# The sixteen matmuls of the masked products with r, alternating between the two column halves of TensorE's array

## The chip, the cores and the metric

The kernel runs on one core of one Trainium2 chip. Five engines work side by side: TensorE (PE in the profile, with its weight loads listed as PEld), VectorE (DVE), ScalarE (ACT), GpSimd (POOL) and SyncE (SP), which here issues all the DMAs. The metric is the device time of one execution in microseconds; less is better.

## The reference

The input passes through a recurrence, and then through two feed-forward blocks. The recurrence is, for 4 batches x 8 heads and for each of 768 steps (head size 40):

```
y[:, :, t] = einsum('bhd,bhde->bhe', rt, state)
Sa = einsum('bhde,bhe->bhd', state, at)
state = state * wt[:, :, None, :] - einsum('bhd,bhe->bhde', Sa, bt) + einsum('bhd,bhe->bhde', vt, kt)
...
x = y as [3072, 320];  h = (x @ w1) * (x @ w2) @ w3;  x = h @ w_out
h = maximum(x @ w_in, 0);  out = (h * h) @ w_out2
```

Inputs are float32 (the weights of the feed-forward blocks arrive in 64 bits and are cut to float32 on the chip).

## The kernel before, in words

The recurrence runs in 24 chunks of 32 steps (`C = 32`), one after the other, all 32 pairs of batch and head at once. What a chunk needs that does not depend on the state is prepared six chunks ahead. The state is then carried from chunk to chunk by six stages of TensorE, each of which writes one PSUM tile that another engine empties before the next stage can run:

- `do_x0` (matmuls at L723): state times a; ScalarE empties it (L725).
- `do_sa` (L733): times the inverse of a triangular matrix; ScalarE empties it (L735).
- `do_sat` (L740): transposes; ScalarE empties it (L742) into the tile `vs`. For a pair of heads `vs` holds 104 rows (two heads of 40, the second from row 64 on) by 64 columns: 32 steps of v and 32 steps of Sa.
- `do_l` (L753), the stage that is changed: for each of 16 pairs of heads one float32 matmul, with 104x64 of `vs` as the weights and 104x64 of r (`RT`: 32 steps for each of the two heads) as the moving operand. The 64x64 products go through a causal mask on VectorE (L755) into rows 64 to 127 of the tile `YI`.
- `do_z` (L763): the state transposed; ScalarE empties it (L766).
- `do_ys` (L778): for each of the 32 heads the products of `YI` with `YR`, 40 columns of weights, 72 moving columns. They give the chunk's output (L790) and the next state (L786). Two heads of a pair go to two column halves of the array.

A float32 matmul appears in the trace as two records, each with its own weight load, so a block of 16 such matmuls has 32 records. A transpose appears as one.

All stages of the recurrence take their PSUM tile from one pool of two buffers, `psat()`, in turn. A stage therefore waits until the tile of the stage but one before it has been emptied. Before the change `do_l` takes two tiles, one for each 8 pairs; `do_z` comes two tiles after the first of them, and so takes that one's buffer.

Between the stages TensorE is given other work, so that it does not stand idle while another engine empties a tile: `Fill.pull(gap)` takes matmuls from a list until their estimated time has reached the gap's. In the first four chunks the list holds the product that folds two weights into one (L455); later it holds the first feed-forward block, 256 tokens for every two chunks (L366 `ab` and L424 `px`). One `ab` tile is emptied by ScalarE (`a_sb`, L397) and VectorE (`g`, L398), and there are two `ab` tiles. The preparation six chunks ahead (`prep_pq` at L578, `prep_kb` at L595, the scans `suf` L539 and `wi` L549 on VectorE) goes between the stages as well, and after every fourth preparation VectorE solves four chunks' triangular matrices in 31 pairs of instructions (`tmp` L637, `T` L640). After the recurrence comes the second feed-forward block (L366 `ph`, L971 `po`).

The order on TensorE is the program's own (`manual_schedule`). The order on the other engines and in the DMA queue is set by a scheduler that simulates a timeline and goes by priorities.

Of the kernel before, what the change touches and what calls it, by code (L numbers as in the profile page):

```python
# [7 lines left out]
F32 = mybir.dt.float32  # L8
F32R = mybir.dt.float32r
# [7 lines left out]
C = 32  # L17
# [8 lines left out]
LEAST, MOST = 0.25, 2.0  # the decays that the recurrence by chunks is meant for  # L26
# the order of the work on what the first chunks need: before the recurrence, and between its stages
# [4 lines left out]
BETWEEN = {  # by chunk and stage  # L32
# [16 lines left out]
FOLD_NS = 535  # of a product of the fold  # L49
# [4 lines left out]
# nanoseconds of other work after each stage of a chunk: x0, sa, sat, l, z, pq, kb, ys  # L54
# [13 lines left out]
FIRST, SECOND = 40000, 20000  # priorities over what comes earlier in the program  # L68
TWIN = [list(range(4 * i, 4 * i + 4)) for i in range(NCH // 4)]  # chunks solved together


class Fill:
    """Work that goes between the stages of the recurrence, in order, with about how long it holds the tensor engine."""
# [6 lines left out]
    def push(self, *items, before=None):  # L80
        """Items of (ns, function, kind); ahead of the first one of a kind, if there is one."""
        at = next((i for i, it in enumerate(self.q) if it[2] == before), len(self.q))
        for it in items:
            self.q.insert(at, it)
            at += 1
# [14 lines left out]
def general(tc, raw, w1, w2, w3t, wo, win, wo2, ident, out):  # L100
    """The same for any decays: the recurrence step by step, and the rest in float32."""
# [3 lines left out]
    with (  # L105
# [59 lines left out]
        with tc.tile_pool(name="g_w", bufs=1) as wp:  # L165
            is64 = w1.dtype != F32

            def fetch(dst, src):
                """Rows of a weight in float32."""
# [73 lines left out]
def body(tc, img, rv, rd, vn, vp, raw, w1, w2, w3t, wo, win, wo2, ident, maskt, out, dbg=None):  # L243
# [4 lines left out]
    with (  # L248
# [5 lines left out]
        X2_d = dram.tile([NCH, 128, DM], F32, name="X2_d")  # per chunk (batch, channel % 32), (channel // 32, step)  # L254
# [6 lines left out]
        with right, tc.manual_schedule(engines={mybir.EngineType.PE}):  # L261
            wp = right.enter_context(tc.tile_pool(name="wp", bufs=1, side="right"))
            wf_ = {n: wp.tile([128, 8, DM], F32R, name="wp" + n) for n in "hl"}  # the folded weight
# [6 lines left out]
            def staged(pl, tags):  # L270
                """The raw weights that come first lie where the first product will need the space."""
                slots, n = staging.setdefault(tags, (deque(), [0]))
                if not slots:
                    t = pl.tile([128, 4, 512], U32, name="early", tag=tags[n[0] % len(tags)])
                    n[0] += 1
                    slots.extend(t[:, i] for i in range(4))
                return slots.popleft()
# [12 lines left out]
            hold = []  # the end of the first window's solution: what follows on that engine waits for its turn  # L290
            count = {"fold": 0, "split": 0}  # raw weights so far
            bufs = {"raw": WB[0], "wst": WB[1], "split": WB[2]}

            def fetch(pl, K, N, parts, dst=None, tag="fold"):
                """[128, K, N] of a weight in float32; one of 64 bits is cut to it from its bits."""
# [26 lines left out]
                # as float32 the upper word has an eighth of the exponent: less 112 it is that of the float32, and  # L322
                # what is below float32's range comes close to zero by itself
# [10 lines left out]
            def split_w(pl, src, h, l, j, k):  # L334
                """Rows 128*k.. and columns 256*j.. of a [320, .] weight as a float32r sum."""
# [5 lines left out]
            def split_r(pl, two):  # L341
                """Rows 256.. of two blocks of 256 columns as float32r sums, their terms above one another: the first
                one's upper term in the lower half, the second one's in the upper half."""
# [25 lines left out]
            def a_tile(n):  # L369
                """The tokens of two chunks."""  # L370
# [68 lines left out]
            def fold(solved):  # L439
                """The weights of the first product; the steps of the fold, in pieces of 256 rows of the transposed w3."""  # L440
# [49 lines left out]
            with (  # L490
# [21 lines left out]
                def first(c, name, shape, places):  # L512
                    """A tile of a preparation; the first ones lie where later tiles will, so that they don't wait."""
# [21 lines left out]
                def prep_scan(c):  # L535
# [8 lines left out]
                    # one too small for an inverse, which `within` doesn't let pass, counts as 1  # L544
# [58 lines left out]
                TT = {}  # L603

                def solve(k, blocks):
                    """All of T by substitution, or the blocks of 16 on its diagonal alone, both at once."""
# [10 lines left out]
                    def view(x):  # L617
                        """Rows and columns of each block; the second one lies 16 rows and 16 columns on."""
# [41 lines left out]
                def corner(c, i):  # L660
                    """The block below the diagonal: - T_22 P_21 T_11, transposed, in two steps."""
# [85 lines left out]
                def do_l(c):  # L747
                    """The masked products of V_s and of SA_s with R_t."""
                    vs = vs_t.pop(c)
                    for g in range(2):  # L750
                        ps = psat()
                        for i in range(8):
                            mm(out=ps[64:128, 0, 64 * i:64 * i + 64], lhsT=vs[0:104, 8 * g + i], rhs=RT[0:104, :, 8 * g + i],  # L753
                               start=True, stop=True, tile_position=(0, 64))
                        dve.tensor_tensor(out=YI[64:128, 16 * g:16 * g + 16, 0:C],  # L755
                                          in0=ps[64:128, 0].rearrange("p (u t) -> p u t", t=C),
                                          in1=msk[64:128].unsqueeze(1).to_broadcast([64, 16, C]), op=ALU.mult)

                def do_z(c):
                    """The state, decayed over the chunk, with the rows and columns exchanged."""  # L760
# [82 lines left out]
                RT = at.tile([128, 2, 16, C], F32, name="RT", tag="rt")  # of each parity in a column of its own  # L843
# [95 lines left out]
        with (  # L939
# [39 lines left out]
            NW = 8  # pieces of the decays  # L979
# [3 lines left out]
            def look(i):  # L983
                """The least and the largest of a piece of the decays."""
# [6 lines left out]
            def within():  # L991
                """1 where all decays are such that the products of a chunk's and their inverses are far from the ends
                of the range, and 0 elsewhere."""
# [41 lines left out]
def layout(r, k, v, w, a, b, moe_w1, moe_w2, moe_w3, moe_w_out, moe2_w_in, moe2_w_out):  # L1035
    import numpy as np

    def e2(x):
        # [chunk, (parity, channel) padded to 104 rows, batch, head pair, step]
# [49 lines left out]
```

## Time and profile before

| | |
|---|---|
| three runs | 1135.08, 1135.51 and 1135.98 us, median 1135.51 |
| span of the profiled execution, first to last instruction | 1131.3 us |
| around the span (median less span) | 4.2 us |
| TensorE busy | 952.6 us (84%) |
| VectorE busy | 745.7 us (66%) |
| L753, matmuls of `do_l` | 768 records, 57.8 us busy |
| L778, matmuls of `do_ys` | 1536 records, 57.4 us busy |

Busy time is the time in which at least one instruction of the kind is under way. Matmuls overlap, so the time that a block of them holds TensorE is read from the start of its first record to the start of the next other matmul, not from the records' own durations. The granted clock (PEclk) is given as a share of 2.4 GHz; its two levels are 1.2 and 2.4 GHz.

### The profile page before, as it was taken

The page shows a single profiled execution, that of the slowest core. Times are in us where ns is not written, and L with a number is a line of the kernel's source. Part 1 is how long each engine was busy: PE and PEld are TensorE (multiplying, and loading weights), DVE is VectorE, ACT ScalarE, POOL GpSimd, SP SyncE. Part 2 cuts the span into 40 slices and gives each one's busy share as a digit, 9 for nine tenths or more (in the row PEclk, how much of TensorE's full clock was granted, in tenths as well). Part 3 has the DMA queues.
Part 4 walks back from the last instruction along what each step waited for, and adds up shares of the span by engine and source line. Part 5 has one row for each costly group of instructions (what it writes and reads, how often), then busy time and mean ns, then how long its engine had stood idle before and what let it go on. Part 6 is the DMA issues. An engine that isn't in the chain of part 4 may idle for free.

```text
span 1131.3 us, 29668 instructions
## 1 busy us (share of the span) xinstructions
PE 952.6 (84%) x12240; PEld 856.6 (76%) x12240; DVE 745.7 (66%) x1467; ACT 453.5 (40%) x1022; POOL 273.8 (24%) x310
## 2 busy tenths in 40 slices
PE   1336776688979889978899998988989999999995
PEld 1235554577879888978789898877778998889985
DVE  6795799965885796678569543789943434343332
ACT  3433655442424333333334343667433433343331
POOL 0383557622132122112210000487400000000000
PEclk9999788898999898988999998999999999999998
DMA  8878666475566655645664453449600200000000
GB/s 209 262 214 219 189 168 189 115 196 146 131 151 160 170 142 140 181 117 150 154 147 111 105 116 87 101 144 201 160 24 1 52 1 24 1 24 1 22 3 26
DMA packets 212677, 134.47 MB, mean 119 GB/s; under 512 B 142974, under 2 KB 187135, under 8 KB 210495
## 3 DMA queue, kind: packets, MB, share of 16 engines
q1 hardware_dynamic: 212535, 132.51, 46.0%
q8 instruction: 98, 1.61, 0.6%
q14 instruction: 44, 0.36, 0.1%
HBM read 99.27 MB, written 33.19 MB: 117 GB/s over the span
## 4 chain that ended last, share of the span: by engine, by line
PE 48%; DVE 26%; DMA 13%; issue 6%; ACT 3%; SPq 2%; POOL 1%; DVEq 0%; ACTq 0%; POOLq 0%
PE po L971 13%; PE ph L366 12%; PE ab L366 10%; DMA im<-img 8%; PE px L424 4%; PE pat L753 3%; DVE tmp L637 3%; DVE T L640 3%; DVE wst L329 3%; DVE wst L327 2%; DVE suf L539 2%; PE pat L763 2%; DVE wi L549 2%; PE pat L778 1%; DVE yst L790 1%
## 5 line engine op out<-in xcount | busy, mean ns | idle before, releaser
L971 PE MATMUL po<-wuh,rh 128*128 128x320 f32 x384 | 118.6, 310 | 5.8 <-DVE ob L976 4.4
L971 PE MATMUL po<-wul,rh 128*128 128x320 f32 x384 | 118.4, 310 | 0.0
L971 PE MATMUL po<-wuh,rl 128*128 128x320 f32 x384 | 113.8, 310 | 4.9 <-DVE rl L958 4.9
L565 POOL TENSOR_TENSOR im<-im,suf 104x256 f32<-104x256 f32 x80 | 74.1, 951 | 135.2 <-DVE suf L539 96.8
L403 ACT CAST gh<-g 128x256 fp32r<-128x256 f32 x96 | 38.9, 405 | 115.7 <-DVE g L398 115.3
L331 POOL TENSOR_TENSOR wst<-wst,raw 128x256 f32<-128x256 f32 (+1 forms) x72 | 67.3, 943 | 60.3 <-DVE wst L329 28.6
L366 PE MATMUL ab<-xh,w1h 128*128 128x256 f32 x192 | 61.5, 320 | 24.1 <-DVE g L398 24.1
L971 PEld LDWEIGHTS po<-wuh,rh 128*128 128x128 f32 x384 | 72.6, 189 | 10.2 <-issue 4.9
L366 PE MATMUL ph<-xh,wih 128*128 128x512 f32 x192 | 76.5, 398 | 1.7 <-POOL wst L331 1.7
L971 PEld LDWEIGHTS po<-wuh,rl 128*128 128x128 f32 x384 | 71.4, 189 | 6.5 <-DVE rl L958 5.9
L366 PE MATMUL ph<-xl,wih 128*128 128x512 f32 x192 | 76.1, 397 | 0.0
L366 PE MATMUL ph<-xh,wil 128*128 128x512 f32 x192 | 76.1, 396 | 0.0
L971 PEld LDWEIGHTS po<-wul,rh 128*128 128x128 f32 x384 | 72.6, 189 | 3.9
L753 PE MATMUL pat<-RT,vs 104*64 104x64 f32 x768 | 57.8, 241 | 17.9 <-ACT vs L742 10.6
L753 PEld LDWEIGHTS pat<-RT,vs 104*64 104x64 f32 x768 | 53.8, 154 | 22.5 <-ACT vs L742 12.2
L640 DVE TENSOR_TENSOR T<-T,tmp 128x31 f32<-128x31 f32 (+20 forms) x170 | 68.1, 400 | 3.1
L637 DVE TENSOR_TENSOR tmp<-PT,T 128x31 f32<-128x31 f32 (+20 forms) x170 | 68.0, 400 | 3.0
L424 PE MATMUL px<-wph,gh 128*128 128x320 f32 x192 | 64.6, 337 | 5.5 <-ACT gh L403 5.5
L778 PE MATMUL pat<-YI,YR 128*40 128x72 f32 (+1 forms) x1536 | 57.4, 237 | 10.6 <-DVE qt L583 8.3
L778 PEld LDWEIGHTS pat<-YI,YR 128*40 128x40 f32 x1536 | 53.1, 125 | 15.0 <-DVE qt L583 9.3
L398 DVE TENSOR_TENSOR g<-a_sb,ab 128x256 f32<-128x256 f32 x96 | 39.8, 415 | 36.3 <-ACT a_sb L397 35.1
L397 ACT COPY a_sb<-ab 128x256 f32<-128x256 f32 x96 | 35.6, 370 | 70.3 <-PE ab L366 69.9
(531 smaller groups left out, 2605.9 us busy)
## 6 DMA issues: line engine op xcount, KB each, us to landing
im<-img SPq DMA_DIRECT2D x38, 322.7 KB
raw<-w3t SPq DMA_DIRECT2D x32, 256.0 KB
KB_d<-kn SPq DMA_DIRECT2D x24, 320.0 KB
YR<-KB_d SPq DMA_DIRECT2D x48, 160.0 KB
AW_d<-wi SPq DMA_DIRECT2D x24, 214.5 KB
wt<-AW_d SPq DMA_DIRECT2D x24, 214.5 KB
raw<-wo SPq DMA_DIRECT2D x16, 320.0 KB
RX<-vp SPq DMA_DIRECT2D x24, 208.0 KB
```

Of the source, the lines that this page charges most:

```text
L331: pool.tensor_tensor(out=o, in0=o, in1=hi.bitcast(F32), op=ALU.mult)
L366: mm(out=ps, lhsT=seq[i][0], rhs=seq[i][1], start=(i == 0), stop=(i == 7))
L397: act.copy(out=a_sb, in_=ps[:, 0])
L398: dve.tensor_tensor(out=g, in0=a_sb, in1=ps[:, 1], op=ALU.mult)
L403: act.copy(out=t["gh"][:, ff], in_=g)
L424: mm(out=ps, lhsT=a_, rhs=b_, start=(k == 0 and i == 0), stop=(k == 7 and i == 2))
L565: eng.tensor_tensor(out=kb[:, g, :, :, j], in0=kb[:, g, :, :, j], in1=sg, op=ALU.mult)
L637: dve.tensor_tensor(out=tv, in0=Pv[:, :, s, s + 1:n].unsqueeze(3).to_broadcast(sh), in1=Tv[:, :, s, 0:s + 1].unsqueeze(2).to_broadcast(sh) ...
L640: return dve.tensor_tensor(out=o, in0=o, in1=tv, op=ALU.subtract).ins
L753: mm(out=ps[64:128, 0, 64 * i:64 * i + 64], lhsT=vs[0:104, 8 * g + i], rhs=RT[0:104, :, 8 * g + i], start=True, stop=True, tile_position=( ...
L778: mm(out=ps[64 * y:64 * y + D, b, 72 * z:72 * z + n], lhsT=YR[:, u], rhs=YI[:, u, 0:n], start=True, stop=True, tile_position=(0, 64 * y))
L971: mm(out=po[j][g], lhsT=a_, rhs=b_, start=(ff == 0 and i == 0), stop=(ff == 15 and i == 2))
```

## The change

The two tiles of `do_l` become one, in one PSUM bank. Matmul i goes to column half i modulo 2 of the array: the even ones write PSUM rows 0 to 63, the odd ones rows 64 to 127, and matmuls 2j and 2j+1 write the same 64 columns of the bank. VectorE still runs two mask instructions for each chunk, of 64x512 elements each, one for each half of the rows; both write rows 64 to 127 of `YI`, so the first one now moves its data from rows 0-63 to rows 64-127. Each of them needs matmuls from the whole block. One tile less is taken from the pool for each chunk.

```
                     vs = vs_t.pop(c)
-                    for g in range(2):
-                        ps = psat()
-                        for i in range(8):
-                            mm(out=ps[64:128, 0, 64 * i:64 * i + 64], lhsT=vs[0:104, 8 * g + i], rhs=RT[0:104, :, 8 * g + i],
-                               start=True, stop=True, tile_position=(0, 64))
-                        dve.tensor_tensor(out=YI[64:128, 16 * g:16 * g + 16, 0:C],
-                                          in0=ps[64:128, 0].rearrange("p (u t) -> p u t", t=C),
-                                          in1=msk[64:128].unsqueeze(1).to_broadcast([64, 16, C]), op=ALU.mult)
+                    ps = psat()
+                    for i in range(16):
+                        q = 64 * (i % 2)
+                        mm(out=ps[q:q + 64, 0, 32 * i - q // 2:32 * i - q // 2 + 64], lhsT=vs[0:104, i], rhs=RT[0:104, :, i],
+                           start=True, stop=True, tile_position=(0, q))
+                    yl = YI[64:128].rearrange("p (i q y) f -> p q i y f", q=2, y=2)
+                    for q in range(2):
+                        r = slice(64 * q, 64 * q + 64)
+                        dve.tensor_tensor(out=yl[:, q, :, :, 0:C],
+                                          in0=ps[r, 0].rearrange("p (i y t) -> p i y t", y=2, t=C),
+                                          in1=msk[r].unsqueeze(1).unsqueeze(1).to_broadcast([64, 8, 2, C]), op=ALU.mult)
```

The lines after `do_l` move down by three (the masks are L758, `do_z` is L766, `do_ys` L781). The rest of the diff takes comments out.

On TensorE the order of the instructions stays as it was; what changes is what they wait for. In chunk 7 before, with the semaphores that a row waits for:

```order
L753 MATMUL pat<-RT,vs 64x64 [waits DMAHW4_49,DMAHW5_49,DMAHW3_49,Activation_49]
L753 MATMUL pat<-RT,vs 64x64 x7
L753 MATMUL pat<-RT,vs 64x64 [waits PE_49]
L753 MATMUL pat<-RT,vs 64x64 x7
...
L763 MATMUL pat<-idt,RX 104x40 [waits DVE_49]
...
L366 MATMUL ab<-xh,w1h 128x256 [waits DVE_49]
```

And in the changed kernel, at the same place:

```order
L753 MATMUL pat<-RT,vs 64x64 [waits DMAHW4_49,DMAHW5_49,DMAHW3_49,Activation_49]
L753 MATMUL pat<-RT,vs 64x64 x15
...
L766 MATMUL pat<-idt,RX 104x40 [waits PE_49]
...
L366 MATMUL ab<-xh,w1h 128x256 [waits DVE_49]
```

The transposes of `do_z` no longer wait for VectorE (the first mask); the first matmul of the next `ab` tile waits for VectorE (a `g`) as before.

On VectorE in chunk 7, before (T and tmp are the solution's steps, YI the masks, g the product that empties an `ab` tile):

```order
L640 TENSOR_TENSOR T<-T,tmp 128x8x24
L755 TENSOR_TENSOR YI<-pat,msk 64x16x32
L637 TENSOR_TENSOR tmp<-PT,T 128x175
L755 TENSOR_TENSOR YI<-pat,msk 64x16x32
L640 TENSOR_TENSOR T<-T,tmp 128x7x25
L398 TENSOR_TENSOR g<-a_sb,ab 128x256
```

And in the changed kernel:

```order
L640 TENSOR_TENSOR T<-T,tmp 128x8x24
L637 TENSOR_TENSOR tmp<-PT,T 128x175
L640 TENSOR_TENSOR T<-T,tmp 128x7x25
L758 TENSOR_TENSOR YI<-pat,msk 64x8x2x32 x2
L637 TENSOR_TENSOR tmp<-PT,T 128x156
L398 TENSOR_TENSOR g<-a_sb,ab 128x256
```

The two masks now stand together and after the next pair of the solution; `g` stands behind both of them, as before, with one more step of the solution ahead of it.

The scheduler has also moved other work. The largest moves are in the opening, on ScalarE between the preparation of chunk 6 and the stages of chunk 1 (kn is the preparation's copy, X, SA and vs the stages' copies; wst, raw and early are raw weights being cut to float32, w1h a weight's upper part). Before:

```order
L599 COPY kn<-pat 128x8x40 x2
L725 ACTIVATE X<-pat 128x320
L324 ACTIVATE wst<-raw 128x256
L325 ACTIVATE raw<-raw 128x256
L735 COPY SA<-pat 128x8x40
L745 COPY YI<-SA 32x8x40 x4
L324 ACTIVATE wst<-raw 128x256
L742 COPY vs<-pat 104x4x4x32
```

And in the changed kernel:

```order
L324 ACTIVATE wst<-early 128x256
L325 ACTIVATE early<-early 128x256
L599 COPY kn<-pat 128x8x40 x2
L725 ACTIVATE X<-pat 128x320
L338 CAST w1h<-wst 128x256
L324 ACTIVATE wst<-early 128x256
L324 ACTIVATE wst<-raw 128x256
L325 ACTIVATE early<-early 128x256
L325 ACTIVATE raw<-raw 128x256
L735 COPY SA<-pat 128x8x40
L745 COPY YI<-SA 32x8x40 x4
L338 CAST w2h<-wst 128x256
```

Work on weights that arrive by DMA now stands ahead of the copies of chunk 1's stages.

## Rows read from the trace of the kernel before

**Rows 1.** Span and mean granted clock of the core.
```profile
core 0: 1131.3 us, clock 0.945
```

**Rows 2.** Stretch, length, busy us of PE, PEld, DVE, ACT, POOL; clock, DMA share, GB/s.
```profile
80.00:230.00 150.00, 108.77 (x1839) 85.47 (x1838) 125.42 (x248) 76.83 (x203) 89.22 (x106) 0.84 0.64 174
230.00:716.00 486.00, 437.84 (x7570) 407.19 (x7569) 336.57 (x757) 175.13 (x410) 81.08 (x89) 0.94 0.55 139
```

**Rows 3.** Chain that ended last: start us, us, what.
```profile
230.65 2.02 PE pat L753 x32
...
374.95 6.64 DMA im<-img
...
493.72 3.61 PE pat L753 x32
...
706.54 2.01 PE pat L753 x32
```

**Rows 4.** TensorE's timeline in chunk 10: start, us, instruction.
```profile
391.43 2.08 PE L753 MATMUL pat<-RT,vs 104*64 104x64 f32 x32
393.43 0.38 PE L366 MATMUL ab<-xh,w1h 128*128 128x256 f32 x1
...
395.06 1.01 PE L763 MATMUL pat<-idt,RX 40*104 40x40 f32 x16
396.00 0.39 PE L366 MATMUL ab<-xl,w2h 128*128 128x256 f32 x1
...
400.58 2.20 PE L778 MATMUL pat<-YI,YR 128*40 128x72 f32 x64
402.71 0.42 PE L424 MATMUL px<-wph,gh 128*128 128x320 f32 x1
```

**Rows 5.** TensorE's timeline at the lower clock, in chunks 2 and 14.
```profile
175.35 4.07 PE L778 MATMUL pat<-YI,YR 128*40 128x72 f32 x64 [5.27 <-DVE qt L583]
179.35 1.92 PE L455 MATMUL pw<-wo_sb,wst 128*128 128x320 f32 x3
...
493.65 3.68 PE L753 MATMUL pat<-RT,vs 104*64 104x64 f32 x32
497.26 0.58 PE L366 MATMUL ab<-xl,w1h 128*128 128x256 f32 x1
```

**Rows 6.** All masks: instructions, durations ns (least, median, largest), first and last start.
```profile
L755 DVE TENSOR_TENSOR YI<-pat,msk x48: 690/695/696, 87.1 to 708.8; 64x512 f32<-64x512 f32 x48
```

**Rows 7.** Groups on VectorE, 230 to 716 us: busy us, mean ns | idle before.
```profile
L786 DVE TENSOR_TENSOR RX<-pat,gc 40x320 f32<-40x320 f32 x76 | 37.0, 487 | 12.9 <-PE pat L778 11.5
...
L790 DVE TENSOR_TENSOR yst<-pat,wt 40x256 f32<-40x256 f32 x80 | 33.8, 422 | 1.8 <-PE pat L778 0.2
```

**Rows 8.** Waits of TensorE, 240 to 720 us: total us, times, longest.
```profile
PE ab L366 <- DVE g L398: 19.9, 9, 4.1
PE pat L753 <- ACT vs L742: 6.6, 4, 4.1
PE pat L763 <- DVE YI L755: 6.4, 2, 3.4
```

**Rows 9.** TensorE's timeline in chunk 7.
```profile
319.57 1.01 PE L763 MATMUL pat<-idt,RX 40*104 40x40 f32 x16 [3.01 <-DVE YI L755]
...
321.97 0.41 PE L366 MATMUL ab<-xh,w1h 128*128 128x256 f32 x1
```

**Rows 10.** VectorE's timeline in chunks 7 and 10.
```profile
319.92 0.69 DVE L755 TENSOR_TENSOR YI<-pat,msk 64x512 f32<-64x512 f32 x1
...
321.02 0.42 DVE L398 TENSOR_TENSOR g<-a_sb,ab 128x256 f32<-128x256 f32 x1
...
394.42 0.42 DVE L398 TENSOR_TENSOR g<-a_sb,ab 128x256 f32<-128x256 f32 x1
```

**Rows 11.** Chain that ended last, in the opening.
```profile
108.10 4.38 DMA early<-w
```

**Rows 12.** ScalarE's timeline in chunk 1.
```profile
103.72 0.46 ACT L725 ACTIVATE X<-pat 128x320 f32<-128x320 f32 x1
```

## The prediction

> **What bounds the kernel now.** I read the span first, then the busy times by stretch, the chain that ended last, TensorE's timeline round the changed block, and TensorE's waits. The span is 1131.3 us at a mean clock of 0.945 [rows 1]; the median of the runs is 1135.5, so 4.2 us lie around the span, which the change doesn't touch, and a gain in the span is taken off the median one for one. The reader should see two regimes in the recurrence. From 80 to 230 us (chunks 0 to 3) VectorE is busy 125 of 150 us and TensorE 109, at a clock of 0.84; from 230 to 716 (chunks 4 to 23) TensorE is busy 438 of 486 and VectorE 337 [rows 2]. So in the second stretch TensorE's own time counts, and the chain that ended last says the same: the changed block L753 is on it as a whole in 17 of the 20 chunks, from 230.65 to 706.54, 15 times with 2.0 us and twice, the one at 493.72 among them, with 3.6 [rows 3], together 37.4 us. The three chunks where it isn't are 7, 11 and 15, in which VectorE, late with the triangular solution, is on the chain instead. In chunks 0 to 3 the chain runs through VectorE, ScalarE and DMAs, and not through this block as a whole.
>
> **The change part by part.**
>
> Matmuls. A block has 32 records. At the full clock it holds TensorE from 391.43 to 393.43, 2.00 us or 62.5 ns a record [rows 4]; at the lower one, 1.2 GHz, from 493.65 to 497.26, 3.61 us or 113 ns [rows 5]. The trace doesn't show this shape alternating between column halves, but it shows the nearest relative: L778 has all its weights' rows in use, 72 moving columns, and goes to the two halves in turn. It takes 2.13 us for 64 records, 33.3 ns each [rows 4], though it streams more columns than L753. At the lower clock it takes 4.00 us, 62.5 ns each [rows 5]. So a record in one half runs beside one in the other. By columns (64 of 72) L753 would come to 29.6 ns; without that credit to 33.3. I take 32, since its weights have 64 columns to L778's 40: 1.02 us a block, 0.98 less. At the lower clock 55.6 to 62.5 ns; with 58 a block is 1.86 us, 1.75 less. On the chain this makes 15 x 0.98 + 2 x 1.75 = 18.2 us. From below the gain is bounded by a pace set by the weights, from above by 29.6 ns, 15 x 1.05 + 2 x 1.83 = 19.4 us.
>
> For the pace of weights: L778 loads 40 columns in 33.3 ns, 1.2 columns a nanosecond. If that is what limits it, 64 columns take 53.3 ns, a block 1.71 us, and the gain is 0.29. Against this speak the transposes L763, which load 104 columns and move 40 in 0.94 us for 16, 59 ns each [rows 4]: at least 1.8 columns a nanosecond, with which 64 columns take 36 ns. At 36 ns a block is 1.15 us and the sum still 15 x 0.85 + 2 x 1.75 = 16.3.
>
> There is a rule against the change. The Trainium skill, "TensorE: Matmul & The Clock Gate", section "Part 3: Packing small matmuls — row/col tiling", says that a weight load overlaps a running matmul only when the two use different row groups. Both halves here use all the rows, so by the rule nothing would overlap; L778, which has the same rows in both halves, disagrees by its 33.3 ns, and I go by it. What the rule would do is priced among the rivals from rows.
>
> Masks. Two instructions of 64x512 before, two after, 0.695 us each [rows 6]. The new form has one stride more, and one of the two moves its data between row halves. L786, which also moves half its data between rows, takes 487 ns for 320 elements, 1.52 ns each; L790, which doesn't, 422 ns for 256, 1.65 each [rows 7]; so nothing shows a price on moving. By these rates 512 elements come to between 0.69 (as now) and 0.84 us; I take 0.695. Before, the first mask could start when half the block was done, 1.0 us in; now both wait for the whole block, which ends at the same 1.0 us, so the second ends at about 1.0 + 1.4 = 2.4 us after the block's start in place of 2.0 + 0.7 = 2.7. `do_ys`, which needs them, comes 9.2 us after the block's start, at 400.58 [rows 4], and hides either.
>
> PSUM buffers. One tile less per chunk shifts the turn: `do_z` no longer waits for the first mask. Before, it did so in chunks 7 and 11, 6.4 us in all [rows 8]; in chunk 7 by 3.01 us, until 319.57 [rows 9]. That wait goes, but it doesn't become gain. Next late is the first matmul of an `ab` tile, at 321.97 [rows 9], which needs a `g` that on VectorE stood behind the second mask and ended at 321.44 [rows 10]. Its place in VectorE's order is the same in the changed kernel, and VectorE, not TensorE, is late there. So TensorE waits some 4 us for `g` in place of 3 for the mask, and gains 0.5 us in each of the two chunks: 1.0 us.
>
> What comes late next in the other chunks. With TensorE 1 us earlier, VectorE's `g` has 1 us less to spare. Where the solution's steps are between, VectorE gets to it late: in chunk 10 it ends at 394.84, 3.4 us after the block's start [rows 4, 10]. The instructions ahead of it are much the same in the changed kernel, so there it can't be much earlier. By the order of instructions nine of the 17 blocks lie in chunks that carry such steps (6, 8, 10, 12, 14, 16, 18, 19, 20). I take off half the gain there, between none and all of the 0.98: 9 x 0.45 = 4 us.
>
> The DMA for the next preparation (6.64 us at 374.95, on the chain [rows 3]) starts when TensorE has read the buffer that it fills, after this block in the same chunk; so it moves forward with TensorE, and what waits for it too.
>
> The opening. VectorE, busy 84% of it [rows 2], does the same work; the masks' place among the other instructions shifts by three at most. On ScalarE, weights now stand ahead of chunk 1's copies X, which ran at 103.72 [rows 12], and SA. I cost this at nothing, because VectorE's work hides it, with 5 us to either side: about one landing of such a weight, 4.38 us [rows 11].
>
> Sum: 18.2 + 1.0 - 4 = 15.2 us less, 1135.5 - 15.2 = 1120.3, so 1120.
>
> **The rivals.**
>
> The weights set the pace, at 1.2 columns a nanosecond. For it: L778's 33.3 ns fits it as well as it fits two halves of 72 columns each. Against: the transposes' 59 ns for 104 columns. Price: 15 x 0.29 + 2 x 1.75 = 7.9, plus 1, less some 2 for VectorE: 1128.5.
>
> The gain stays only where VectorE has no solution to do. For it: `g` already costs TensorE 19.9 us in nine waits [rows 8]. Then all nine blocks named above give nothing, and the other eight (chunks 4, 5, 9, 13, 17, 21, 22 and 23) 7 x 0.98 + 1.75 = 8.6: 1127. Against: several of those waits follow from TensorE's own earlier work, as the DMA's does, and so move with it.
>
> Nothing runs side by side, since one half's matmul must be through before the other's starts, though their weights load ahead as now. Then a block keeps its 2.0 us and the time is 1135. Against: L778.
>
> The other side, first: the opening's order. ScalarE stands at the head of its queue for an early weight's DMA and then for POOL's part of it, before X, SA and vs of chunk 1, and the like in chunks 2 and 3. At 4.38 us a landing [rows 11] and up to three such stops a chunk in two chunks that is 26 us at worst, against a gain of 15; it decides if more than three stops are not hidden. With five, 22 - 15 = 7 us slower: 1142. Against: the DMA queue issues those weights earlier too, and VectorE's backlog from about 135 us on gives TensorE time to catch up.
>
> The other side, second: switching halves for each matmul stops the next weights from being loaded under the running matmul. Price: L763 adds up as loading and moving one after the other, 144 columns in 59 ns, 2.4 a nanosecond; 64 columns of weights then add 27 ns to the 62.5, a block takes 2.86 us, and 17 x 0.86 = 15 us are lost: 1150. It decides as soon as more than half the 27 ns can't be hidden by two halves. This is what the page's rule would mean here. L778's pace denies it.
>
> **How the numbers follow.** Forecast 0.60; weights' pace 0.10; gain only where VectorE is free 0.15; nothing 0.04; the opening 0.08; weights in series 0.03. A measurement of this kernel can tell 0.2%, 2.3 us, from no change. Faster: nearly all of the first three, 0.84; same 0.05; slower 0.11. The likeliest case's own range is 1112 to 1127: the upper bound of the matmuls with no loss to VectorE and 4 us from the opening at one end, all the loss and a few microseconds in the opening at the other. The range of 8 in 10 is 1109 to 1133: it takes in the two smaller gains with the opening's 5 us, and leaves out no change and both slower cases (0.15) and what lies under 1109.
>
> **What would show it.** L753's block from its start to the next matmul: 1.0 us bears out the two halves, 1.7 the weights' pace, 2.0 or more neither. The masks at 0.7 us, both behind the block. No wait of `do_z` for a mask, and in chunks 7 and 11 a longer one of `ab` for `g`. TensorE's waits for `g` in all: near 24 us as forecast, over 30 if VectorE takes the gain. Chunk 4's block starting near 230 us if the opening is neutral, at 235 or later if not. The last block near 690 in place of 706, with all behind it moved by as much. The forecast is wrong if the block shrinks to 1 us and the last chunk doesn't come at least 10 us earlier, or if the block doesn't shrink.

## The result, and the profile after

| kernel | median of its runs, us | lowest to highest | ratio to before, 95% interval |
|---|---|---|---|
| before | 1135.74 | 1135.08 to 1138.80 (4 runs) | |
| changed | 1122.69 | 1116.81 to 1124.22 (4 runs) | 0.9854 [0.9823, 0.9884] |
| changed, again, beside other runs of before | 1122.32 | 1118.58 to 1123.72 (6 runs) | 0.9842 [0.9809, 0.9875] |

By the first measurement the kernel is faster by 1.2 to 1.8%, and the forecast of 1120 us stands 2.7 below its median. The profiled execution of the changed kernel took 1124.05 us, and this is its span (in [rows 1] before):

```profile
core 0: 1122.0 us, clock 0.941
```

The spans differ by 9.3 us and the medians by 13. In the changed kernel's run 2.0 us lie around the span (1124.05 less 1122.0). The 4.2 us that the forecast put there for before were more than that, so a part of them was probably scatter, the profiled execution of before being itself quicker than the median. One pair of traces can therefore not say where each microsecond of the median went; it can show which waits and blocks changed.

By stretch, with the columns of [rows 2]:

```profile
80.00:230.00 150.00, 104.20 (x1840) 80.63 (x1840) 125.19 (x251) 76.11 (x204) 90.45 (x107) 0.85 0.65 177
230.00:706.00 476.00, 424.99 (x7581) 394.04 (x7581) 337.25 (x755) 175.33 (x411) 79.94 (x88) 0.93 0.57 141
```

TensorE is busy 13 us less from 230 us on, and VectorE as long as before. The granted clock of the stretch was 0.93 against 0.94, so TensorE's other work is likely to have taken a little longer in this execution. The second stretch is cut at 706 us because the recurrence now ends some 10 us earlier.

TensorE's timeline in chunk 10 (start, us, instruction, and in brackets the idle time before it and what ended it), against [rows 4]:

```profile
388.97 1.15 PE L753 MATMUL pat<-RT,vs 104*64 104x64 f32 x32 [0.22 <-ACT vs L742]
390.05 0.39 PE L366 MATMUL ab<-xh,w1h 128*128 128x256 f32 x1
...
391.68 1.01 PE L766 MATMUL pat<-idt,RX 40*104 40x40 f32 x16
...
397.53 2.20 PE L781 MATMUL pat<-YI,YR 128*40 128x72 f32 x64 [0.26 <-DVE qt L583]
```

The block holds TensorE from 388.97 to 390.05, 1.08 us for the same 32 records that took 2.00. The relatives L766 and L781 (L763 and L778 before) are unchanged. At the lower clock, in chunk 14, against 3.61 us in [rows 5]:

```profile
487.27 1.98 PE L753 MATMUL pat<-RT,vs 104*64 104x64 f32 x32
489.18 0.58 PE L366 MATMUL ab<-xl,w1h 128*128 128x256 f32 x1
```

That is 1.91 us. In the whole second stretch, chunks 4 to 23, the blocks, each from its start to the next matmul, add up to 43.4 us before and 23.8 after, 19.6 less. In the chain that ended last, the line "PE pat L753" falls from a share of 3.3% to one of 1.7%.

The masks, all 48 of them (durations least, median and largest in ns, then first and last start), cost what they did in [rows 6]:

```profile
L758 DVE TENSOR_TENSOR YI<-pat,msk x48: 683/690/695, 88.7 to 697.5; 64x512 f32<-64x512 f32 x48
```

The waits of TensorE from 240 to 720 us (total us, times, longest), against [rows 8]:

```profile
PE ab L366 <- DVE g L398: 30.3, 13, 4.1
PE pat L723 <- DVE RX L789: 7.4, 3, 4.2
PE pat L753 <- ACT vs L742: 6.4, 4, 4.0
```

No wait of `do_z` (L766 now) for a mask is left there; it had 6.4 us in two waits. The waits for `g` rose by 10.4 us. Both together were 26.3 us and are 30.3. The waits for RX were 2.5 us, and a wait of 5.5 us for `gh` (L403), which stood in this list before, is gone. How the one turned into the other is seen in chunk 7, first on TensorE and then on VectorE, against [rows 9, 10]:

```profile
309.79 1.15 PE L753 MATMUL pat<-RT,vs 104*64 104x64 f32 x32
...
312.49 1.01 PE L766 MATMUL pat<-idt,RX 40*104 40x40 f32 x16
...
318.68 0.58 PE L366 MATMUL ab<-xh,w1h 128*128 128x256 f32 x1 [4.03 <-DVE g L398]
```

```profile
316.43 1.39 DVE L758 TENSOR_TENSOR YI<-pat,msk 64x512 f32<-64x512 f32 x2
317.85 0.32 DVE L637 TENSOR_TENSOR tmp<-PT,T 128x156 f32<-128x156 f32 x1
318.20 0.42 DVE L398 TENSOR_TENSOR g<-a_sb,ab 128x256 f32<-128x256 f32 x1
```

The transposes L766 no longer wait 3.01 us for the mask; they run at once, and TensorE stops 4.03 us later in the row, at the `ab` tile whose `g` stands behind the masks and the solution's steps on VectorE.

How far the recurrence is ahead, from the start of the changed block in chunks 4 and 23 (230.65 and 706.54 for the first chunk and the last in [rows 3]):

```profile
231.41 1.15 PE L753 MATMUL pat<-RT,vs 104*64 104x64 f32 x32 [1.07 <-ACT vs L742]
...
695.61 1.15 PE L753 MATMUL pat<-RT,vs 104*64 104x64 f32 x32
```

It enters the second stretch 0.8 us later and leaves it 10.9 us earlier. ScalarE in chunk 1 shows where the opening loses it, against [rows 12]:

```profile
103.39 0.43 ACT L324 ACTIVATE wst<-early 128x256 f32<-128x256 f32 x1 [5.38 <-DMA early<-w]
...
104.89 0.46 ACT L725 ACTIVATE X<-pat 128x320 f32<-128x320 f32 x1
...
107.61 0.41 ACT L735 COPY SA<-pat 128x320 f32<-128x320 f32 x1
```

ScalarE stands 5.38 us at an early weight ahead of X, which runs at 104.89 in place of 103.72. The stop costs so little because ScalarE stood there before, too, for another DMA, ahead of the copies kn:

```profile
103.08 0.75 ACT L599 COPY kn<-pat 128x320 f32<-128x320 f32 x2 [4.69 <-DMA KB_d<-kn]
```

With the weights that now stand ahead of SA, chunk 1's block starts at 112.17 in place of 109.52. And in chunks 1 and 2 the transposes after the block now wait for its masks, which they didn't before; TensorE's timeline:

```profile
122.30 1.58 PE L766 MATMUL pat<-idt,RX 40*104 40x40 f32 x16 [6.29 <-DVE YI L758]
...
161.26 1.58 PE L766 MATMUL pat<-idt,RX 40*104 40x40 f32 x16 [3.27 <-DVE YI L758]
```

In chunk 1 they ran at 119.43 before, in chunk 2 at 162.85. So chunk 1 is later by 2.9 us here, and chunk 2 no longer. The waits for the masks replace one in the middle of the block, until ScalarE's x (L678) had freed the buffer for the second of its two tiles; the changed kernel doesn't have it. Before, in chunks 1 and 2:

```profile
109.52 1.12 PE L753 MATMUL pat<-RT,vs 104*64 104x64 f32 x16
114.43 1.97 PE L753 MATMUL pat<-RT,vs 104*64 104x64 f32 x16 [3.80 <-ACT x L678]
...
156.24 1.97 PE L753 MATMUL pat<-RT,vs 104*64 104x64 f32 x16 [3.47 <-ACT x L678]
```

### The profile page after: what moved, and what is told of

It reads as the page before. It is cut to its first block, busy times and chain, and to the rows that moved or that the text cites. A ratio compares the mean times of both kernels' runs of the same rounds, so it can differ in the third digit from the quotient of the medians.

```text
span 1122.0 us, 29683 instructions
## 1 busy us (share of the span) xinstructions
PE 935.7 (83%) x12240; PEld 838.4 (75%) x12240; DVE 745.8 (66%) x1467; ACT 452.1 (40%) x1022; POOL 274.1 (24%) x310
## 4 chain that ended last, share of the span: by engine, by line
PE 48%; DVE 22%; DMA 17%; issue 5%; ACT 3%; SPq 2%; POOL 1%; DVEq 0%; ACTq 0%; POOLq 0%
PE po L974 13%; PE ph L366 13%; DMA im<-img 10%; PE ab L366 9%; PE px L424 4%; DVE tmp L637 3%; DVE T L640 3%; DVE wst L329 2%; PE pat L781 2%; DVE wst L327 2%; PE pat L753 2%; DVE suf L539 2%; PE pat L766 2%; DMA X_d<-yst 1%; DMA xf<-X_d 1%
## 5 line engine op out<-in xcount | busy, mean ns | idle before, releaser
L403 ACT CAST gh<-g 128x256 fp32r<-128x256 f32 x96 | 38.9, 406 | 111.4 <-DVE g L398 111.0
L974 PEld LDWEIGHTS po<-wuh,rh 128*128 128x128 f32 x384 | 73.0, 190 | 10.9 <-issue 5.1
L781 PE MATMUL pat<-YI,YR 128*40 128x72 f32 (+1 forms) x1536 | 57.8, 238 | 14.9 <-DVE qt L583 8.0
L781 PEld LDWEIGHTS pat<-YI,YR 128*40 128x40 f32 x1536 | 53.5, 126 | 19.7 <-DVE qt L583 9.3
L366 PEld LDWEIGHTS ab<-xh,w1h 128*128 128x128 f32 x192 | 39.4, 205 | 36.4 <-DVE g L398 34.8
L404 DVE TENSOR_TENSOR gl<-g,gh 128x256 fp32r<-128x256 f32 x96 | 47.4, 494 | 27.0 <-ACT gh L403 26.7
L424 PE MATMUL px<-wph,gl 128*128 128x320 f32 x192 | 61.2, 319 | 1.3 <-DVE gl L404 1.3
```

The lines of the kernel that those rows point to most:

```text
L366: mm(out=ps, lhsT=seq[i][0], rhs=seq[i][1], start=(i == 0), stop=(i == 7))
L403: act.copy(out=t["gh"][:, ff], in_=g)
L404: dve.tensor_tensor(out=t["gl"][:, ff], in0=g, in1=t["gh"][:, ff], op=ALU.subtract)
L424: mm(out=ps, lhsT=a_, rhs=b_, start=(k == 0 and i == 0), stop=(k == 7 and i == 2))
L781: mm(out=ps[64 * y:64 * y + D, b, 72 * z:72 * z + n], lhsT=YR[:, u], rhs=YI[:, u, 0:n], start=True, stop=True, tile_position=(0, 64 * y))
L974: mm(out=po[j][g], lhsT=a_, rhs=b_, start=(ff == 0 and i == 0), stop=(ff == 15 and i == 2))
```

## The experiments

The time of before differed between the groups of runs (medians from 1134.0 to 1140.1 us), so kernels are compared by their ratio to the runs of before beside them.

| kernel | median us (lowest to highest) | ratio to before, 95% interval | median block, us |
|---|---|---|---|
| e1_one_half | 1130.87 (1127.66 to 1142.25) | 0.9959 [0.9940, 0.9978] | 2.01 |
| e2_two_banks | 1116.41 (1115.34 to 1119.68) | 0.9836 [0.9815, 0.9857] | 1.08 |
| e2b_two_banks_again | 1115.05 (1108.94 to 1119.14) | 0.9848 [0.9810, 0.9886] | 1.08 |
| e3_block_twice | 1140.84 (1137.01 to 1143.40) | 1.0031 [1.0008, 1.0053] | 2.02 |
| e7_half_columns | 1144.34 (1143.12 to 1146.17) | 1.0069 [1.0052, 1.0085] | 1.99 |
| e8_four_quarters | 1116.63 (1115.00 to 1118.25) | 0.9862 [0.9810, 0.9914] | 1.03 |
| e9_two_quarters | 1119.66 (1115.25 to 1124.07) | 0.9889 [0.9830, 0.9948] | 1.72 |
| e0_after_again | 1122.32 (1118.58 to 1123.72) | 0.9842 [0.9809, 0.9875] | 1.08 |
| e4_masks_behind_g | 1121.61 (1120.04 to 1125.94) | 0.9841 [0.9808, 0.9874] | 1.08 |
| e5_before_no_solution | 1107.79 (1104.59 to 1113.53) | 0.9707 [0.9665, 0.9749] | 2.01 |
| e6_after_no_solution | 1089.95 (1087.06 to 1091.98) | 0.9552 [0.9512, 0.9591] | 1.08 |
| e11_half_of_gl_on_pool | 1117.86 (1114.41 to 1123.59) | 0.9869 [0.9834, 0.9904] | 1.08 |

The diffs are against the changed kernel; the one of the solution's steps was made to the kernel before as well. A block is that of the masked products, from its first record to the next matmul on TensorE (its line is L752 to L755, by kernel).

**The buffer turn without the alternation.** One tile for the chunk, as in the change, but all 16 matmuls in the upper half.

```
-  q = 64 * (i % 2)
-  mm(out=ps[q:q + 64, 0, 32 * i - q // 2:32 * i - q // 2 + 64], ..., tile_position=(0, q))
+  mm(out=ps[64:128, i // 8, 64 * (i % 8):64 * (i % 8) + 64], ..., tile_position=(0, 64))
...
+  for g in range(2):
+      dve.tensor_tensor(out=YI[64:128, 16 * g:16 * g + 16, 0:C], in0=ps[64:128, g]..., op=ALU.mult)
```

> One PSUM tile per chunk as in the changed kernel, but all 16 matmuls in the upper column half as before (8 in each of the tile's two banks); one mask per bank. This undoes the alternation and keeps the new turn of the PSUM buffers. Theory A (the gain is TensorE time, from two halves side by side): the block stays at 2.0 us, and the time is that of the kernel before within 4 us, 1132 to 1139; the transposes' wait for a mask in chunks 7 and 11 is gone and stands before an ab matmul instead. Rival B (the gain comes from the freed buffer turn): 1121 to 1127, with a block of 2.0 us.

TensorE's timeline in chunk 10:

```profile
392.21 2.08 PE L752 MATMUL pat<-RT,vs 104*64 104x64 f32 x32 [0.22 <-ACT vs L742]
394.22 0.39 PE L366 MATMUL ab<-xh,w1h 128*128 128x256 f32 x1
```

The block is back at 2.01 us, so the one tile does nothing for its pace. Yet the time falls by 4.7 us (2.5 to 6.8, from the ratio and 1136.6), more than the forecast gave the buffer turn; 1130.87 us lies between the two ranges that were expected. The scheduler made a new order on the other engines for this kernel, too (in the opening ScalarE's stop for an early weight is not in it), so the 4.7 us are not shown to be the turn's alone. Its profiled execution took 1142.25 us, far above its own median, so the trace can't tell where these microseconds come from. What the alternation adds to it is the ratio of the two ratios: 0.9854 / 0.9959 = 0.9895 and, by the second measurement, 0.9842 / 0.9959 = 0.9883, some 12 to 13 us, each uncertain by about 4.

**The bank.** The odd matmuls write to the tile's second bank.

```
-  mm(out=ps[q:q + 64, 0, 32 * i - q // 2:...
+  mm(out=ps[q:q + 64, i % 2, 32 * i - q // 2:...
-  in0=ps[r, 0]...
+  in0=ps[r, q]...
```

> The changed kernel, but the odd matmuls write the tile's second bank, so that the halves never share a bank. Theory A with the bank without effect: block 1.08 us (1.05 to 1.11) and 1119 to 1126 as in the changed kernel. Rival C (the shared bank costs some of the pace, 33.8 ns a record where L778's by columns would be 29.6): block 0.95 to 1.0 us and 1 to 3 us less.

```profile
388.57 1.15 PE L753 MATMUL pat<-RT,vs 104*64 104x64 f32 x32 [0.16 <-ACT vs L742]
389.65 0.38 PE L366 MATMUL ab<-xh,w1h 128*128 128x256 f32 x1
```

The block (chunk 10 again) is 1.08 us with one bank or two. Since the time came out a little lower, the kernel was run again:

> The two halves in two banks, again, since its first times were some 6 us under the changed kernel's with the same block of 1.08 us. If that was the run-to-run spread of the clock: ratio to before within 0.002 of the changed kernel's 0.984, 1117 to 1124 us. If the bank matters outside the block: 0.980 or less.

With 0.9848 it can't be told from the changed kernel. No cost of the shared bank shows.

**Does TensorE's time reach the end?** The whole block is done twice.

```
-  for i in range(16):
+  for i in 2 * list(range(16)):
```

> The changed kernel with the 16 matmuls of the block issued twice over, the same results written again. What the second 32 records add to the block is the pace without what lies at a block's ends: theory A expects 0.95 to 1.05 us more (30 to 33 ns a record), block 2.03 to 2.13. The time tells how much of a microsecond of TensorE in this place reaches the end: with the 0.6 to 0.75 that the changed kernel's gain suggests, 24 x 1.0 x 0.6 to 0.75 = 14 to 18 us more than the changed kernel, 1135 to 1141. Rival B (order and buffers, not TensorE time): within 4 us of the changed kernel, 1119 to 1127.

```profile
347.00 2.09 PE L753 MATMUL pat<-RT,vs 104*64 104x64 f32 x64
349.01 0.38 PE L366 MATMUL ab<-xl,w2h 128*128 128x256 f32 x1
```

The 32 added records take 2.02 - 1.08 = 0.94 us, 29.4 ns each; the other 0.14 us of the block belong to its two ends. The time rises to 1.0031 from 0.9842 or 0.9854, which is 20 to 22 us of 1136.6, uncertain by about 4, for about 19 us of added work in chunks 4 to 23 (20 x 0.94, and more where the clock is lower). That is more than the 14 to 18 us expected: in this kernel nearly all that the block takes shows at the end.

The other kernels don't all give the same price, though. e1_one_half holds TensorE as long as this one (2.01 and 2.02 us a block), and its ratio is lower by 0.0072, 8 us (5 to 12). e7_half_columns (1.99 us) takes 24 to 26 us more than the changed kernel, again more than its 12 to 18. e9_two_quarters, whose block is 0.64 us longer than the changed kernel's, some 13 us in 20 chunks, takes only 4 to 5 us more, uncertain by about 8, in two runs of 1115.25 us at a clock of 0.957 and 1124.07 at 0.943. So TensorE's time in this block counts, but a microsecond of it was not worth the same in each kernel. The scheduler's order, made anew for each, and the granted clock may stand between; they were not separated.

**What sets 29.4 ns: weights or moving columns?** Each matmul is cut in two with 32 moving columns each; all 64 columns of weights are loaded for both.

```
+  for y in range(2):
      for i in range(16):
...
-         mm(out=ps[q:q + 64, 0, ...:... + 64], lhsT=vs[0:104, i], rhs=RT[0:104, :, i],
+         o = 32 * i - q // 2 + 32 * y
+         mm(out=ps[q:q + 64, 0, o:o + 32], lhsT=vs[0:104, i], rhs=RT[0:104, y, i],
```

> The changed kernel with each matmul cut in two of 32 moving columns (first those of all even heads, then those of the odd ones), weights the same and loaded for each: 64 records of half the columns, the same weights twice as often. Theory A (moving columns set the pace, two halves side by side): 64 x 15 to 18 ns = 0.96 to 1.15 us and something at the ends, block 1.05 to 1.25, time within 5 us of the changed kernel. Rival D (the weights, or a floor per record, set the 33 ns): block 2.1 to 2.2 us, 12 to 18 us more than the changed kernel.

```profile
345.59 2.06 PE L755 MATMUL pat<-RT,vs 104*64 104x32 f32 x64
347.58 0.39 PE L366 MATMUL ab<-xl,w2h 128*128 128x256 f32 x1
```

If the ends of a block cost the same 0.14 us here, it is (1.99 - 0.14) / 64 = 28.9 ns a record with half the moving columns. They don't set the pace. What is left is either a floor for any record or the weights' 64 columns. Two kernels with 32 columns of weights in each matmul tell these apart. In the first the four quarters of the array take turns, in the second only two at a time:

```
-  for i in range(16):
+  for i, h in ((2 * j + p, 32 * g) for j in range(8) for g in range(2) for p in range(2)):   # four quarters
+  for h, i in ((32 * g, i) for g in range(2) for i in range(16)):                            # two quarters
...
+  r = slice(q + h, q + h + 32)
-  mm(out=ps[q:q + 64, 0, ...], lhsT=vs[0:104, i], ..., tile_position=(0, q))
+  mm(out=ps[r, 0, ...], lhsT=vs[0:104, i, h:h + 32], ..., tile_position=(0, q + h))
```

> The changed kernel with each of the 16 matmuls cut in two of 32 weight columns (v and Sa apart), the moving operand the same, going round the four column quarters in turn. Nothing is left out. The last set left two readings of the pace: a record takes 29 ns whether it moves 64 columns (twice over: 0.94 us for 32 records more) or 32 (1.99 us for 64). Reading W (weights of 64 columns are loaded one after the other, 2.2 columns a ns): with 32 columns a record takes 14 to 19 ns, block 1.0 to 1.35 us. Reading F (some 29 ns for every record whose weights use all rows): block 1.95 to 2.05.

> As the run before, but first all 16 halves with v, in the first and third quarter in turn, and then all 16 with Sa, in the second and fourth. So two quarters alternate, with half the weight columns and all 64 moving ones. Reading W alone (the weights set the pace): as with four quarters, 1.0 to 1.35 us. If two tiles side by side are bound by the moving columns as well (62.5 ns for one tile alone, 29 to 31 for two), block 1.9 to 2.1 us: then the changed block meets both bounds at once.

TensorE's timeline in chunk 10 of the kernel with four quarters, and in chunk 11 of the one with two:

```profile
390.15 1.10 PE L755 MATMUL pat<-RT,vs 104*32 104x64 f32 x64
391.18 0.39 PE L366 MATMUL ab<-xh,w1h 128*128 128x256 f32 x1
```

```profile
408.27 1.79 PE L755 MATMUL pat<-RT,vs 104*32 104x64 f32 x64
410.00 0.39 PE L366 MATMUL ab<-xl,w1h 128*128 128x256 f32 x1
```

With four quarters a record takes (1.03 - 0.14) / 64 = 13.9 ns, so there is no floor near 29. Reading W fits this: 64 / 28.9 and 32 / 13.9 are 2.2 and 2.3 columns a nanosecond. But with two quarters a record takes (1.72 - 0.14) / 64 = 24.7 ns, between the two forecasts, where W gives 13.9. So half the weights' columns alone bring 29.4 down to 24.7, and going from two tiles in turn to four brings 24.7 down to 13.9.

One half alone takes (2.01 - 0.14) / 32 = 58.4 ns. That leaves a second reading: a tile has a turn of its own, and the tiles in turn share it. Half of 58.4 is 29.2, what the changed block takes; two quarters make a turn of 2 x 24.7 = 49.4 ns, and a quarter of that is 12.4, a little under the 13.9 of four. The moving columns don't set such a turn by themselves, as they are 64 in one half and in two quarters (58.4 and 49.4). The changed block meets both bounds at once, 28.9 by W and 29.2 by the turn. Which of them holds in it, and what makes up the turn, was not tried.

**Does VectorE's order take back the gain?** The changed kernel was run beside the next three.

> The changed kernel again, beside the next three on one chip. 1117 to 1125 us, 10 to 19 less than the kernel before.

It gave the same ratio as at first, within the intervals. Then the masks were put behind the newest `g` on VectorE, since they have until `do_ys`:

```
...
-  stage(do_z, c, gap=gaps[4])
+  stage(do_z, c)
+  with tc.issue_after(newest[0]) if newest else nullcontext():
+      stage(do_m, c)
+  fill.pull(gaps[4])
```

> The changed kernel with the two masks of a chunk put behind the newest g on VectorE (they are emitted after the state's transposes and may not be issued before that g). Nothing is left out. Theory A (the part of the gain that is missing stands in TensorE's waits for g, which VectorE reaches late, behind masks that nobody needs yet): TensorE's waits for g fall from 28 us to 20 to 24, the wait of 4.0 us in chunk 7 to under 3, and the time is 3 to 6 us less than the changed kernel's, 1116 to 1120. Rival E (VectorE's whole work in those chunks sets the pace, and the order within it doesn't matter, as what is put back is waited for later): within 2 us of the changed kernel.

The waits of TensorE from 232 to 715 us, of the changed kernel in this second measurement and of this one:

```profile
PE ab L366 <- DVE g L398: 28.7, 12, 4.3
```

```profile
PE ab L367 <- DVE g L399: 30.1, 12, 5.5
```

Neither the time nor the waits for `g` fall. In chunk 7, where the masks do stand behind that `g` now, its wait goes from 4.05 to 3.37 us, not under 3, and in chunk 9 another grows to 5.54. The masks ahead of `g` are at most a small part of what makes it late.

**Is it the triangular solution?** For chunks 4 to 23 only the first of its 31 pairs of steps is left, once in the kernel before and once in the changed one (the diff is the same). Both kernels leave out work of the solution.

```
-  items += [lambda s=s: step(s) for s in range(n - 1)]
+  items += [lambda s=s: step(s) for s in range(n - 1 if blocks == 2 else 1)]
...
-  return [it() for it in solve(k, blocks)][C // blocks + 3]
+  return [it() for it in solve(k, blocks)][C // blocks + 3 if blocks == 2 else 6]
```

> The kernel before, with 30 of the 31 pairs of VectorE's steps of the triangular solution left out for chunks 4 to 23 (the transposes round them stay). It is the base for the next one. TensorE's waits for g fall under 10 us from 20; 1105 to 1130 us.

> The changed kernel with the same steps of the solution left out. Theory A (those steps are what takes back part of the gain): the change is now worth 16 to 21 us against the run before this one, nearly 20 chunks x 0.93 and two slow blocks. Rival F (other waits, on DMAs or ScalarE, take it back as well): 13 us or less, as with the solution in place.

The same row of waits, without the change and with it:

```profile
PE ab L366 <- DVE g L398: 12.6, 7, 3.5
```

```profile
PE ab L366 <- DVE g L398: 15.1, 11, 3.3
```

The solution's steps make about half of the waits for `g` (they fell to 12.6 us and not under 10), but nothing shows that they take the gain: without them the change is worth 1107.79 - 1089.95 = 17.8 us, and with them, in the same group of runs, 1140.10 - 1122.32 = 17.8 us. By the intervals of the ratios the first is uncertain by some 6 us and the second by 4, so a share of a few microseconds could hide in them. All waits of TensorE together from 232 to 690 us rise from 47.2 to 49.2 us with the change (52.2 in its second profile), and from 39.2 to 43.2 where the steps are left out: 2 to 5 us, with or without them.

**A lighter VectorE.** Half of the subtractions `gl`, in the tiles of the recurrence, go to POOL.

```
-  dve.tensor_tensor(out=t["gl"][:, ff], ...)
+  (pool if ff % 2 and n < 9 else dve).tensor_tensor(out=t["gl"][:, ff], ...)
```

> The changed kernel with the lower terms gl of the odd ab tiles (L404, some 0.45 us on VectorE, 36 of them up to the ninth pair of chunks) computed by POOL, which is busy 83 of 480 us there. Nothing is left out. If VectorE's load in the chunks with the solution takes back part of the gain, as the pair without the solution showed (17.8 us in place of 13): TensorE's waits for g fall from 28 us to under 22, 3 to 8 us less than the changed kernel, 1115 to 1120. If POOL's work slows VectorE's (they were seen to stretch each other: steps of the solution of 0.33 to 1.28 us beside POOL's) or gl comes late for px: 1121 or more.

The waits for `g` fall from 28 to 24.2 us (232 to 700 us), and the ratio, 0.9869, is no better than the changed kernel's. No version that does all the work clearly beats the changed kernel.

## Why the prediction was right, and where it was not

**The bound.** Right. That TensorE's own time counts from 230 us on is what the block done twice shows: 20 to 22 us for about 19 us of work. The forecast counted 17 of the 20 blocks, since three were not on the chain as a whole; the runs can't tell 17 from 20, and the price of a microsecond differed from kernel to kernel.

**The matmuls.** The mechanism was right: work in one half runs beside work in the other, 29.4 ns a record against 58.4 in one half. The size of the term was nearly right, 1.08 us against 1.02 and 1.91 against 1.86, but its reason was wrong: I scaled L778 by moving columns, and halving them leaves a record at 28.9 ns. That the forecast met it is in part luck, as I had rounded up for the weights' 64 columns. The rival with 1.2 columns a nanosecond falls, since a record takes 29.4 ns and not 53.3; what sets L778's 33.3 ns, from which that rate was read, was not tried. That rival's price had a slip, too: it kept 1.75 us for each of the two slow blocks, where its own rate (62.5 ns for 40 columns at the lower clock, so 100 ns for 64) leaves 0.4. The rivals without overlap and with weights in series fall with the block's 1.08 us. The Trainium skill, "TensorE: Matmul & The Clock Gate", section "Part 3: Packing small matmuls — row/col tiling", lets a weight load overlap a running matmul only in other row groups; here both halves use the same 104 rows, and the block takes 1.08 us in place of 2.01, so the rule isn't borne out. By that rule the loads wouldn't overlap in one half either, so it would have meant a block of 2.0 us still, and not the 2.86 at which the prediction priced it.

**Net of what the alternation brings.** The forecast had 18.2 for the matmuls less 4 for VectorE, 14.2 us; the change against the kernel with the buffer turn alone gives 12 to 13, uncertain by about 4.

**The masks.** Right: 0.69 us each, and TensorE doesn't wait for them after 240 us in the first profile, and once for 1.3 us in the second.

**The buffer turn.** The wait went where the forecast put it: in chunk 7 from 3.01 us for the mask to 4.03 for `g`. But the term was probably mis-sized. It was put at 1.0 us, and the change without the alternation gained 4.7 (2.5 to 6.8). I counted only the two chunks where TensorE waited for a mask; the rest comes from one tile less in other places or from the order that the scheduler made with it, and which is open.

**What VectorE takes back.** The size fits and the cause isn't shown. The waits of `do_z` and for `g` together rose by 4.0 us after 240 us, as the -4 had it, in one execution of each kernel; but the reason given, nine chunks with steps of the solution, isn't borne out, as the change is worth the same without the steps and the waits grow without them as well. The list of these chunks was misread, too: in the trace of before, from a chunk's first stage to the next one's, VectorE runs no instruction of the steps in chunks 8 and 16 and only two and three in 12 and 20. By the mark that I had set, over 30 us of waits for `g` if VectorE takes the gain, the 30.3 us of the first profile (28.7 in the second, from 232 to 715) would have spoken for that rival. It fell all the same, because 6.4 of these microseconds had only moved over from the masks.

**The opening.** Costed at nothing, it costs little: chunk 4's block starts 0.8 us later in the first profile of the changed kernel and 2.4 in the second. In the variants that keep all the work it lies between 229.4 and 233.2 us, 229.25 without the alternation, so part of this is scatter. One stop of ScalarE of the rival's five is seen in the rows above, and the price is at most about a tenth of that rival's 22 us. What I had missed is beside it: the turn of the buffers, which takes the wait of `do_z` for a mask away from 240 us on, brings two such waits into chunks 1 and 2, 9.6 us in all, where VectorE is the late one. They cost little: they stand in place of the 7.3 us (3.80 and 3.47) that TensorE waited inside these blocks before, and chunk 4 starts nearly when it did.

**The end.** The last block came at 695.6 us, and 694.5 in the second profile, in place of 690; that is 10.9 and 12 us earlier than before, just past the 10 us under which the forecast would have been wrong. It is 4.5 to 5.6 us short of the forecast in a single execution, of which 0.8 to 2.4 are the opening's. In the first profile a part can be the clock: 0.93 of 476 us against 0.94 of 486 is, by the two levels, some 67 us at 1.2 GHz against 58, an estimate from the rows by stretch. The second profile had 0.95 up to 706 us, so the clock doesn't explain it there, and the rest can't be put down to a place. The sum of 15.2 us lies inside what the two measurements give, 13 to 20 and 14 to 22 us by their intervals.

## What to carry to other kernels

When matmuls with different weights have at most 64 columns of them and stand one after another in one half of the array, try them in the two halves in turn. A record came to half of what it took in one half alone (29.4 ns against 58.4), so that is the first estimate; its moving columns are not, as half of them changed nothing. With at most 32 columns of weights four quarters in turn were faster a record than two (13.9 ns against 24.7), so the number of tiles in turn counts for more than the size of each. Where a pool of PSUM buffers is small, count the tiles that a change takes out of its turn and measure that alone: here the kernel with that turn and the order that came with it gained 4.7 us of some 17. And a wait that grows behind a removed one has to be counted together with it before it is called a loss.

## What the runs showed of the hardware

Halving the moving columns from 64 to 32 didn't speed up a record (28.9 ns against 29.4). Four column quarters in turn gave 13.9 ns a record and two 24.7, and with four the 64 records of the finer cut took no longer than the 32 of the coarser one, 1.03 us against 1.08. Two column halves that write to one PSUM bank were as fast as two that write to two (1.08 us a block in both). 64 columns of weights and 64 moving ones took 58.4 ns a record in one half alone and 29.4 in two halves in turn, with the same 104 rows.
